# Two blocks of the first layer as one Strassen product in a retention, Mish and SwiGLU kernel

## The chip, the cores and the metric

The kernel runs on one core of a Trainium2 chip. The metric is the time of the program on the device in microseconds (us). Its engines work beside each other, each through its own list of instructions in order: TensorE (PE in the rows, with its weight loads as PEld), VectorE (DVE), ScalarE (ACT), GpSimd (POOL) and SyncE (SP), which issues the transfers (DMA) between the chip's memory and the core's SBUF. TensorE writes its products to PSUM, which has eight banks.

## The reference

What is computed, cut to the formulas. The retention is over 4 x 8 heads of 576 tokens; its output is the 2304 x 512 matrix `x` of the two layers behind it, which have 2048 and 1536 inner columns.

```python
ret = (scale * q @ k.T) * Dmat          # Dmat: gamma ** (i - j) below the diagonal
x = transposed(ret @ v)                 # 2304 tokens x 512
h = x @ w_in                            # first layer, 512 -> 2048
y = (h * tanh(log1p(exp(h)))) @ w_out   # Mish, 2048 -> 512
g = y @ w_gate                          # second layer, 512 -> 1536
out = (g * sigmoid(g) * (y @ w_val)) @ w_out2
```

## The kernel before

**Precision.** All products of the layers are of fp32 numbers in two parts, a high and a low one (type fp32r); a product is three matmuls: high x high, high x low, low x high. So every operand has to be split first: ScalarE copies the high part (a CAST), VectorE (sometimes GpSimd) subtracts it to get the low part. Weights come from memory as `raw` tiles of 128 x 512 64-bit words, out of which `rebias`, `sign` and `join` (lines 105 to 114: one operation of ScalarE, three of VectorE) make fp32 numbers.

**Stages.** The retention comes first, with the first slots of the first layer between its steps. The first layer works through six blocks of 384 tokens (`NB`, `T`); in each, 16 units of 128 inner columns (`F1`). `slot(s)` is unit `s % 16` of block `s // 16`: `g1` makes 12 matmuls of 128 x 384 into a bank `h`, ScalarE applies Mish and casts the high part of `g`, VectorE subtracts for the low part (`g_lo`, line 612), and `g2(s - 4)` makes the 12 matmuls of 128 x 384 of the slot four earlier (`LAG`) into four banks `acc`. A slot has 24 matmuls, and the first layer 96 slots. The weights of all 32 units stay in SBUF from the first block on.

**The second layer** takes two blocks as a pair and makes its first products by Strassen's method: seven products of sums and differences of quarters instead of eight. The quarters of its weights (12 groups of four quarters: `w_gate` and `w_val` in six pairs each) are made ahead, in the first layer's slots: `second(s)` runs one step of `group` and `last` a slot from slot 20 (`PREP`) on, in 14 of each 16 slots, five slots a group. A group loads two `raw` tiles, makes the numbers, forms four sums (line 213), and then `put`s seven quarters: cast, subtraction, and a store to DRAM (`comb`) from a tile `c`, of which there are four. `last` does the same with the second products' weights (`find`, two puts, the subtraction on GpSimd). All loads and stores stand on SP's list in the order of the program. In the second layer `stream` loads the quarters back (`su`), `ysteps` splits the seven combinations of a pair of blocks, and `strassen` makes the seven products of 6 matmuls each into three banks `t` that take turns in two; the second products (`fins`, 128 x 512) are spread between them.

Of the kernel before, what the change touches and what calls it, by code (L numbers as in the profile page):

```python
# [7 lines left out]
F32 = mybir.dt.float32  # L8
# [8 lines left out]
def retention_mish_swiglu(  # L17
# [28 lines left out]
    NA, NBU = 19, 13  # L46
# [3 lines left out]
    PREP = 20  # L50
    EARLY = (9, 11, 14, 17)
# [3 lines left out]
    cl, cr = ExitStack(), ExitStack()  # L55
    wa = cr.enter_context(tc.tile_pool(name="wa", bufs=NA, side="right"))
    dp = ctx.enter_context(tc.tile_pool(name="dp", bufs=1, space=bass.MemoryType.DRAM))
    gp = ctx.enter_context(tc.tile_pool(name="gp", bufs=3))
    xsp = cl.enter_context(tc.tile_pool(name="xsp", bufs=XS))
# [20 lines left out]

    def words(j):
        w = raw[j].rearrange("p (n t) -> p n t", t=2)
        return w[:, :, 0], w[:, :, 1]

    def fetch(lim):
# [5 lines left out]
        raw[j] = xp.tile([128, 2 * DM], U32, tag="raw", name=f"raw{j}", bufs=RAW)  # L91
# [24 lines left out]
    def part(lim, eng=nc.gpsimd):  # L116
# [5 lines left out]
        u = pools["a" if j < NA else "b"].tile([128, 2, DM], F32R, tag="u", name=f"u{j}")  # L122
# [48 lines left out]
    comb = [[dp.tile([128, 2, 2, KH], F32, tag=f"c{i}_{n}", name=f"comb{i}_{n}") for n in range(NG)] for i in range(PAIRS)]  # L171
    find = [dp.tile([128, 2, DM], F32, tag=f"f{i}", name=f"find{i}") for i in range(F2)]

    def raw_load(key, src, whole):
        raw[key] = xp.tile([128, 2 * DM], U32, tag="raw", name=f"raw{key}", bufs=RAW)
# [10 lines left out]
    def group(i, z, stg):  # L186
        keys = [f"{'gv'[z]}{i}_{e}" for e in range(2)]
        if stg == 0:
            for e in range(2):
                raw_load(keys[e], cols((w2_gate, w2_val)[z], 2 * i + e), False)  # L190
            return
        if stg == 1:
            for e in range(2):
                rebias_raw(keys[e])
            return
        if stg == 2:
            for e in range(2):
                sign(keys[e])
                join(keys[e])
            return  # L200
        v = {}
        for e in range(2):
            lo, hi = words(keys[e])
            for n in range(2):
                v[f"a{e + 1}{n + 1}"] = lo[:, n * KH:(n + 1) * KH].bitcast(F32)
                v["1324"[2 * e + n]] = hi[:, n * KH:(n + 1) * KH].bitcast(F32)
        s = {n: v[str(n)] for n in (1, 2, 3, 4)}
        if stg == 3:
            for out_, a, b, op in (
                (s[1], v["a21"], v["a22"], ALU.add), (s[3], v["a11"], v["a21"], ALU.subtract),  # L210
                (s[2], s[1], v["a11"], ALU.subtract), (s[4], v["a12"], s[2], ALU.subtract),
            ):
                nc.vector.tensor_tensor(out=out_, in0=a, in1=b, op=op)
        for c, nm in enumerate(USES):
# [708 lines left out]
```

## Time and profile before

| | us |
|---|---|
| median of three runs | 924.15 |
| lowest, highest | 924.09, 925.74 |
| the profiled execution | 925.63 |
| its span, first to last instruction | 923.5 |
| TensorE busy in it | 913.3 |
| VectorE, ScalarE, GpSimd busy | 514.5, 362.1, 75.5 |

An engine's busy time is the time in which at least one of its instructions runs. Matmuls overlap in a pipeline, so the mean time of one is longer than the step from one to the next. A row of windows gives, for a stretch of the span, the busy time of each engine, the granted clock of TensorE as a share of 2.4 GHz, the busy share of the DMA engines and what they moved.

### The profile page before, as it was taken

The page shows a single profiled execution, that of the slowest core. Times are in us where ns is not written, and L with a number is a line of the kernel's source. Part 1 is how long each engine was busy: PE and PEld are TensorE (multiplying, and loading weights), DVE is VectorE, ACT ScalarE, POOL GpSimd, SP SyncE. Part 2 cuts the span into 40 slices and gives each one's busy share as a digit, 9 for nine tenths or more (in the row PEclk, how much of TensorE's full clock was granted, in tenths as well). Part 3 has the DMA queues.
Part 4 walks back from the last instruction along what each step waited for, and adds up shares of the span by engine and source line. Part 5 has one row for each costly group of instructions (what it writes and reads, how often), then busy time and mean ns, then how long its engine had stood idle before and what let it go on. Part 6 is the DMA issues. An engine that isn't in the chain of part 4 may idle for free.

```text
span 923.5 us, 14629 instructions
## 1 busy us (share of the span) xinstructions
PE 913.3 (99%) x5684; PEld 870.5 (94%) x5684; DVE 514.5 (56%) x950; ACT 362.1 (39%) x729; POOL 75.5 (8%) x71
## 2 busy tenths in 40 slices
PE   9999999999999999999999999999999999999998
PEld 8888899999999999999999999998999998999997
DVE  3778599355656566656635444556444556544444
ACT  3767466344444445444533222223222223222222
POOL 3654200000000000000000000000000000000000
PEclk9999999999999999999999999999999999999999
DMA  9999255045554463454536755544644444644421
GB/s 206 253 247 250 70 180 185 23 149 171 171 171 155 158 198 130 164 189 127 181 138 224 254 206 205 205 160 161 226 160 157 156 162 155 216 158 160 160 69 69
DMA packets 115348, 156.56 MB, mean 170 GB/s; under 512 B 45392, under 2 KB 80976, under 8 KB 115280
## 3 DMA queue, kind: packets, MB, share of 16 engines
q1 hardware_dynamic: 114176, 155.21, 52.3%
q8 instruction: 45, 0.74, 0.3%
q10 hardware_dynamic: 1104, 0.42, 0.2%
q14 instruction: 23, 0.19, 0.1%
HBM read 122.58 MB, written 33.03 MB: 168 GB/s over the span
## 4 chain that ended last, share of the span: by engine, by line
PE 92%; DVE 3%; DMA 2%; ACT 2%; issue 1%; SPq 0%; ACTq 0%; DVEq 0%
PE t L816 28%; PE h L552 21%; PE acc L586 21%; PE fa L742 16%; PE o L455 2%; PE s L379 1%; DMA raw<-in_moe_w_out_dram 1%; DMA raw<-in_moe_w_in_dram 1%; PE idle L500 1%; PE tk L363 1%; PE o L446 1%; DVE p L388 1%; PE state L422 1%; PE tq L332 1%; DVE raw L114 0%
## 5 line engine op out<-in xcount | busy, mean ns | idle before, releaser
L816 PE MATMUL t<-y,su 128*128 128x384 f32 x1512 | 306.5, 338 | 1.0 <-DVE cv L783 1.0
L816 PEld LDWEIGHTS t<-y,su 128*128 128x128 f32 x1512 | 271.4, 188 | 24.4 <-DVE cv L783 2.3
L552 PE MATMUL h<-xs,u 128*128 128x384 f32 x1152 | 215.1, 336 | 0.0
L586 PE MATMUL acc<-g,u 128*128 128x384 f32 x1152 | 214.6, 336 | 0.3 <-DVE u L125 0.3
L586 PEld LDWEIGHTS acc<-g,u 128*128 128x128 f32 x1152 | 201.5, 188 | 0.6 <-DVE u L125 0.6
L552 PEld LDWEIGHTS h<-xs,u 128*128 128x128 f32 x1152 | 200.9, 188 | 0.4
L742 PE MATMUL fa<-fu,g 128*128 128x512 f32 x648 | 190.0, 395 | 0.1
L742 PEld LDWEIGHTS fa<-fu,g 128*128 128x128 f32 x648 | 118.6, 188 | 7.5 <-ACT g L764 0.5
L612 DVE TENSOR_TENSOR g<-m,g 128x384 fp32r<-128x384 f32 x96 | 53.7, 560 | 118.6 <-ACT g L608 118.2
L764 ACT CAST g<-sg 128x384 fp32r<-128x384 f32 x72 | 36.9, 513 | 175.0 <-DVE sg L801 121.4
L603 ACT ACTIVATE m<-h 128x384 f32<-128x384 f32 x96 | 47.0, 490 | 132.7 <-PE h L552 132.4
L790 ACT ACTIVATE sg<-sg 128x384 f32<-128x384 f32 x54 | 28.4, 525 | 96.3 <-DVE sg L783 96.3
L769 DVE TENSOR_TENSOR g<-sg,g 128x384 fp32r<-128x384 f32 x72 | 40.2, 558 | 40.6 <-ACT g L764 40.6
L182 POOL TENSOR_TENSOR f<-rawf,f 128x256 fp32r<-128x256 f32 x24 | 23.7, 1006 | 343.7 <-ACT f L181 343.7
L608 ACT CAST g<-m 128x384 fp32r<-128x384 f32 x96 | 49.4, 514 | 2.6
L783 DVE TENSOR_TENSOR u<-t,p 128x384 f32<-128x384 f32 x36 | 20.1, 557 | 49.8 <-PE t L816 45.6
L783 DVE TENSOR_TENSOR v<-t,p 128x384 f32<-128x384 f32 x36 | 20.0, 556 | 38.1 <-PE t L816 37.4
L801 DVE TENSOR_TENSOR sg<-sg,cv 128x384 f32<-128x384 f32 x54 | 30.2, 559 | 1.9
L114 DVE SCALAR_TENSOR_TENSOR raw<-raw 128x512 uint32<-128x512 uint32 x32 | 27.7, 866 | 0.0
L124 ACT CAST u<-raw 128x512 fp32r<-128x512 f32 x32 | 21.4, 669 | 13.9 <-DVE raw L114 13.8
L110 DVE SCALAR_TENSOR_TENSOR raw<-raw 128x512 uint32<-128x512 uint32 x32 | 26.0, 814 | 0.0
L105 ACT ACTIVATE raw<-raw 128x512 f32<-128x512 f32 x32 | 22.1, 689 | 9.0 <-DMA raw<-in_moe_w_in_dram 4.9
(80 smaller groups left out, 746.1 us busy)
## 6 DMA issues: line engine op xcount, KB each, us to landing
su<-comb SPq DMA_DIRECT2D x126, 512.0 KB, 3.2
comb<-c SPq DMA_DIRECT2D x84, 256.0 KB, 3.5
raw<-in_moe_w_in_dram SPq DMA_DIRECT2D x16, 512.0 KB, 5.1
raw<-in_moe_w_out_dram SPq DMA_DIRECT2D x16, 512.0 KB, 3.9
rawg<-in_moe_w_gate_dram SPq DMA_DIRECT2D x12, 512.0 KB, 6.2
rawf<-in_moe_w_out_dram SPq DMA_DIRECT2D x12, 512.0 KB, 4.7
rawv<-in_moe_w_val_dram SPq DMA_DIRECT2D x12, 512.0 KB, 6.4
find<-f SPq DMA_DIRECT2D x24, 256.0 KB, 2.4
```

Source lines behind the costliest of these rows:

```text
L552: nc.tensor.matmul(ps, lhsT=u[:, a, kk * 128:(kk + 1) * 128], rhs=s[:, e, :], start=(c == 0), stop=(c == n - 1),)
L586: nc.tensor.matmul(accs[b][d][:, :T], lhsT=u[:, a, d * 128:(d + 1) * 128], rhs=g[:, e, :], start=(i == 0 and c == 0), stop=(i == F1 - 1 an ...
L603: nc.scalar.activation(w, hs.pop(s), AF.Mish)
L608: nc.scalar.copy(out=gs[s][:, 0, :], in_=ws[s])
L612: nc.vector.tensor_tensor(out=g[:, 1, :], in0=ws.pop(s), in1=g[:, 0, :].bitcast(F32), op=ALU.subtract)
L742: nc.tensor.matmul(accs["f", b][m], lhsT=gs[u, e, h][:, x, m * 128:(m + 1) * 128], rhs=fu[2 * (u % PAIRS) + e][:, a, :], start=first, stop ...
L764: nc.scalar.copy(out=gs[u, e, h][:, 0, :], in_=x)
L769: nc.vector.tensor_tensor(out=g[:, 1, :], in0=x, in1=g[:, 0, :].bitcast(F32), op=ALU.subtract)
L783: nc.vector.tensor_tensor(out=out_, in0=a, in1=b_, op=ALU.add)
L790: nc.scalar.activation(x, bank_ if part_ is None else x, AF.Silu)
L801: later.append(lambda: nc.vector.tensor_tensor(out=y, in0=y, in1=x, op=ALU.mult))
L816: nc.tensor.matmul(p, lhsT=w[:, n % 2, a, kk * 128:(kk + 1) * 128], rhs=y[:, x, kk, :], start=begin and kk == 0 and (a, x) == (0, 0), stop ...
```

## The change

The first layer's slots stop after four blocks (`NC` = 4, 64 slots instead of 96). The last two blocks are one pair: `pair1(i)`, eight times, takes two units and makes seven Strassen products of 6 matmuls (128 x 384) into banks `te`, then Mish and the split of four results. The second products of a pair of units (`outs`) go into six banks `ea`: for each unit 36 matmuls of 128 x 256 (256 columns of one block, 256 of the other, the remaining 128 of both together) instead of 24 of 128 x 384. They stand in a queue, of which some are made after each Strassen product (`FIN1`); the second products of slots 60 to 63 (`old`) are made the same way during the first pair.

The quarters of the first layer's weights come from the units in SBUF: `group1` adds high and low parts, forms the four sums, puts four quarters through `c` tiles, and stores the other three (`ecomb`) from the unit itself. This preparation and the second layer's is one list (`pieces`): 14 pieces for each of the first eight groups, 10 for each of the last four, 2.6 pieces a slot from slot 20 on (`RATE`) and then 1.15 a Strassen product (`RATE1`). The combinations of the two blocks' tokens (`ye`) are made from slot 51 on, the last three in the first pair. Buffers of units that are no longer needed are taken again by name (`place`) for `ye`, the loaded quarters (`eu`, `su`), the second layer's combinations and its weights (`fu`).

```diff
-    NA, NBU = 19, 13
+    NA = 18
+    NC = 4
+    RATE, RATE1, AHEAD = 2.6, 1.15, 34
...
+    def place(kind, i, shape, dtype, name):
+        j = home[kind, i]
+        return pools["a" if j < NA else "b"].tile(shape, dtype, tag=f"u{j}", name=name)
...
+    def group1(i):
+        v = {}
+
+        def whole():
+            x = rp.tile([128, 2 * DM], U32, tag="raw", name=f"e{i}").bitcast(F32)
+            for e in range(2):
+                u = unit["in", 2 * i + e]
+                for h in range(2):
+                    nm = f"a{e + 1}{h + 1}"
+                    if nm in USES:
+                        m = i * NG + USES.index(nm)
+                        nc.sync.dma_start(
+                            out=comb1[m // 2][:, m % 2], in_=u[:, :, h * KH:(h + 1) * KH].bitcast(F32)
+                        )
+                    v[nm] = x[:, (2 * e + h) * KH:(2 * e + h + 1) * KH]
+                nc.vector.tensor_tensor(
+                    out=x[:, e * DM:(e + 1) * DM], in0=u[:, 0, :].bitcast(F32), in1=u[:, 1, :].bitcast(F32),
+                    op=ALU.add,
+                )
...
+        for n in range(2 * PAIRS):
+            load, bias, whole, sums, puts = gr[n]
+            f_load, f_bias, f_whole, f_puts = last(n)
+            g = group1(n) if n < F1 // 2 else None
+            yield bias
+            yield lambda: (whole(0), f_load())
+            if g:
+                yield g[0]
+            yield lambda: whole(1)
+            if g:
+                yield g[1]
+            yield sums
+            yield lambda: puts(("a11", "a12", "a22"))
+            if g:
+                yield lambda: g[2](("s2", "s3"))
+            yield lambda: puts(("s2", "s3"))
+            yield lambda: (puts(("s1", "s4")), gr[n + 1][0]() if n + 1 < 2 * PAIRS else None)
+            if g:
+                yield lambda: g[2](("s1", "s4"))
+            yield f_bias
+            yield f_whole
+            yield f_puts
...
+            if s >= PREP:
+                second(int((s + 1 - PREP) * RATE))
...
+            for c, (nm, tn, begin) in enumerate(PRODUCTS):
+                if begin:
+                    t[tn] = pha.tile([128, T], F32, tag="h", name=f"te{i}_{tn}")
+                p = t[tn]
+                m = i * NG + c
+                product(p, su["e", m // 2][:, m % 2], ys["e", c], begin)
+                if m % 2:
+                    stream1(m // 2 + len(ring1))
+                new = []
+                if c == 0:
+                    nc.scalar.copy(out=r["p1"], in_=p)
+                elif c == 1:
+                    add(r["u"], p, r["p1"])
+                elif c == 2:
+                    result(0, 0, wt("w"), p)
+                elif c == 3:
+                    r["v"] = wt("v")
+                    add(r["v"], p, r["p1"])
+                else:
+                    e, h, x = ((1, 1, r.get("v")), (1, 0, r["p1"]), (0, 1, r["u"]))[c - 4]
+                    add(x, p, x)
+                    result(e, h, x, x)
+                fins(FIN1[c] if i else 6)
+                while rests:
+                    rests.pop(0)()
+                rests.extend(new)
+                step = i * NG + c
+                if i == 0:
+                    pop(ahead, 2)
+                elif step >= AHEAD:
+                    pop(ahead, 1)
+                second(int((NS - PREP) * RATE + (step + 1) * RATE1))
+
+        FIN1 = (9, 12, 12, 12, 9, 9, 9)
...
+            if s == NS - F1 + 2:
+                ya, yb = ysteps("e", xt[NB - 2], xt[NB - 1])
+                ahead += ya + yb[0] + yb[1]
+            if s > NS - F1 + 2:
+                pop(ahead, 1 + s % 2)
```

The order on VectorE at slots 62 to 64 before (L612 is `g_lo` of a slot, L262 the low part of the next block's tokens, L213 sums and L182 puts of a group):

```order
L612 TENSOR_TENSOR g62_3974<-m62_3972,g62_3974 128x384
L612 TENSOR_TENSOR g63_4008<-m63_4002,g63_4008 128x384
L262 TENSOR_TENSOR xs4_2_4004<-x4_1172,xs4_2_4004 128x384
L262 TENSOR_TENSOR xs4_3_4006<-x4_1172,xs4_3_4006 128x384
L213 TENSOR_TENSOR rawv3_0_3857<-rawv3_1_3859 128x256
L213 TENSOR_TENSOR rawv3_0_3857<-rawv3_0_3857,rawv3_1_3859 128x256
L213 TENSOR_TENSOR rawv3_1_3859<-rawv3_0_3857 128x256
L213 TENSOR_TENSOR rawv3_1_3859<-rawv3_0_3857,rawv3_1_3859 128x256
L182 TENSOR_TENSOR c3_7_4017<-rawv3_0_3857,c3_7_4017 128x256
L182 TENSOR_TENSOR c3_9_4021<-rawv3_0_3857,c3_9_4021 128x256
L182 TENSOR_TENSOR c3_12_4025<-rawv3_1_3859,c3_12_4025 128x256
L612 TENSOR_TENSOR g64_4056<-m64_4054,g64_4056 128x384
```

And in the changed kernel, from the `g_lo` of slot 61 to that of slot 62 and on (L677 is `g_lo`, the tile of two slots bears the even number; L192 are puts of both kinds, L770 the low part of a token combination):

```order
L677 TENSOR_TENSOR g60_4130<-m61_4173,g60_4130 128x384
L192 TENSOR_TENSOR c3_7_4177<-rawv3_0_3961,c3_7_4177 128x256
L192 TENSOR_TENSOR c3_9_4181<-rawv3_0_3961,c3_9_4181 128x256
L192 TENSOR_TENSOR c3_12_4185<-rawv3_1_3963,c3_12_4185 128x256
L192 TENSOR_TENSOR e7_s2_4189<-e7_4087,e7_s2_4189 128x256
L192 TENSOR_TENSOR e7_s3_4193<-e7_4087,e7_s3_4193 128x256
L192 TENSOR_TENSOR c3_8_4197<-rawv3_1_3963,c3_8_4197 128x256
L192 TENSOR_TENSOR c3_10_4201<-rawv3_0_3961,c3_10_4201 128x256
L770 TENSOR_TENSOR ye_3_1_4142<-x5_1404,ye_3_1_4142 128x384
L677 TENSOR_TENSOR g62_4235<-m62_4233,g62_4235 128x384
L192 TENSOR_TENSOR c3_11_4238<-rawv3_0_3961,c3_11_4238 128x256
L192 TENSOR_TENSOR c3_13_4242<-rawv3_1_3963,c3_13_4242 128x256
```

Seven puts in a row now stand between two slots' `g_lo`, where there were three or four, and parts of the token combinations come between them.

ScalarE behind the Mish of slot 63, before (L603 Mish, L608 the high part of `g`, L257 of the tokens, L181 casts of puts):

```order
L603 ACTIVATE m63_4002<-h63_3977 128x384
L257 CAST xs4_2_4004<-x4_1172 128x384
L257 CAST xs4_3_4006<-x4_1172 128x384
L608 CAST g63_4008<-m63_4002 128x384
L181 CAST c3_7_4017<-rawv3_0_3857 128x256
L181 CAST c3_9_4021<-rawv3_0_3857 128x256
L181 CAST c3_12_4025<-rawv3_1_3859 128x256
L603 ACTIVATE m64_4054<-h64_4041 128x384
```

And in the changed kernel, into the first pair (L666 Mish, L673 the high part of `g`, L114 rebias of a raw tile, L191 casts of puts, L921 the copy of the first Strassen product out of its bank, L766 the high part of a token combination, L897 Mish of a result):

```order
L666 ACTIVATE m63_4285<-h63_4260 128x384
L673 CAST g62_4235<-m63_4285 128x384
L114 ACTIVATE rawf7_4085<-rawf7_4085 128x512
L191 CAST f7_0_4293<-rawf7_4085 128x256
L191 CAST f7_1_4297<-rawf7_4085 128x256
L921 COPY scratch_4303<-te0_1_4304 128x384
L766 CAST ye_4_0_4318<-x4_1202 128x384
L766 CAST ye_4_1_4319<-x4_1202 128x384
L114 ACTIVATE rawg4_0_4246<-rawg4_0_4246 128x512
L114 ACTIVATE rawg4_1_4248<-rawg4_1_4248 128x512
L766 CAST ye_5_0_4344<-t2_e_3811 128x384
L897 ACTIVATE we0_4360<-te0_1_4304 128x384
```

The copy that frees the first bank, and the Mish that frees it again, stand behind preparation work that waits for VectorE, for stores and for loads.

## Rows read from the trace of the kernel before

**Rows 1.** Page: busy time of PE, and its granted clock in 40 slices

```profile
PE 913.3 (99%) x5684; PEld 870.5 (94%) x5684; DVE 514.5 (56%) x950; ACT 362.1 (39%) x729; POOL 75.5 (8%) x71
PEclk9999999999999999999999999999999999999999
```

**Rows 2.** Windows: first layer (first row), second layer (second row)

```profile
core 0: us, PE busy (x) PEld busy (x) DVE busy (x) ACT busy (x) POOL busy (x), PEclk, DMA share, GB/s
300.00:400.00 100.00, 100.00 (x577) 100.00 (x577) 59.54 (x117) 49.67 (x108) 8.22 (x9) 1.00 0.49 162
600.00:700.00 100.00, 99.49 (x514) 91.90 (x514) 50.46 (x94) 25.47 (x49) 0.00 (x0) 1.00 0.49 174
```

**Rows 3.** Timeline of PE in the second layer: start, duration, line, shape, count

```profile
702.05 1.22 PE L816 MATMUL t<-y,su 128*128 128x384 f32 x6
703.10 0.86 PE L742 MATMUL fa<-fu,g 128*128 128x512 f32 x3
703.80 1.22 PE L816 MATMUL t<-y,su 128*128 128x384 f32 x6
```

**Rows 4.** Timeline of PE in the retention: full weights, narrow products

```profile
82.97 1.00 PE L446 MATMUL o<-qT,sbd 128*128 128x64 f32 x8
83.91 0.68 PE L455 MATMUL o<-p,vs 64*64 64x64 f32 x16
```

**Rows 5.** Groups of VectorE: line, form, count, busy us, mean ns, idle before

```profile
L612 DVE TENSOR_TENSOR g<-m,g 128x384 fp32r<-128x384 f32 x96 | 53.7, 560 | 118.6 <-ACT g L608 118.2
L182 DVE TENSOR_TENSOR c<-rawv,c 128x256 fp32r<-128x256 f32 x42 | 16.5, 422 | 7.3 <-ACT c L181 7.3
L125 DVE TENSOR_TENSOR u<-raw,u 128x512 fp32r<-128x512 f32 x19 | 13.1, 688 | 1.7 <-ACT u L124 0.9
L262 DVE TENSOR_TENSOR xs<-x,xs 128x384 fp32r<-128x384 f32 x18 | 11.8, 678 | 0.0
L110 DVE SCALAR_TENSOR_TENSOR rawg<-rawg 128x512 uint32<-128x512 uint32 x12 | 10.4, 869 | 0.0
L596 DVE COPY y<-acc 128x384 f32<-128x384 f32 x12 | 6.5, 554 | 6.4 <-PE acc L586 6.3
L213 DVE TENSOR_TENSOR rawg<-rawg,rawg 128x256 f32<-128x256 f32 x12 | 5.1, 423 | 0.2
L106 DVE TENSOR_SCALAR rawg<-rawg 128x512 uint32<-128x512 uint32 x12 | 5.0, 427 | 9.1 <-DMA rawg<-in_moe_w_gate_dram 9.1
```

**Rows 6.** Tile c: its idle-ended lines and landing time of its stores

```profile
  DMA comb<-c: 13.6, 22
DMA to landing us min/median/max: 2.0/3.5/5.9
```

**Rows 7.** Timeline of one group's last puts: the third and fourth wait for stores

```profile
313.94 1.32 SPq L183 DMA_DIRECT2D comb<-c  x3
315.59 0.95 ACT L181 CAST c<-rawv 128x256 fp32r<-128x256 f32 x2
316.77 0.42 ACT L181 CAST c<-rawv 128x256 fp32r<-128x256 f32 x1 [0.23 <-DMA comb<-c]
317.22 0.42 DVE L182 TENSOR_TENSOR c<-rawv,c 128x256 fp32r<-128x256 f32 x1 [0.23 <-ACT c L181]
317.85 0.42 ACT L181 CAST c<-rawv 128x256 fp32r<-128x256 f32 x1 [0.66 <-DMA comb<-c]
```

**Rows 8.** Page, DMA issues: KB each, median us from issue to landing

```profile
comb<-c SPq DMA_DIRECT2D x84, 256.0 KB, 3.5
rawg<-in_moe_w_gate_dram SPq DMA_DIRECT2D x12, 512.0 KB, 6.2
```

**Rows 9.** Groups of ScalarE

```profile
L608 ACT CAST g<-m 128x384 fp32r<-128x384 f32 x96 | 49.4, 514 | 2.6
L181 ACT CAST c<-rawg 128x256 fp32r<-128x256 f32 x42 | 16.2, 423 | 7.4 <-DMA comb<-c 6.0 <-DVE c L182 0.6 <-issue 0.5
```

More of the change, by code (lines that the diff above doesn't have):

```diff
@@ L219, in last, with whole @@
[L219 to L225 removed]
+        def whole(e):
+            sign(keys[e])
+            join(keys[e])
+            lo, hi = words(keys[e])
+            for h in range(2):
+                v[f"a{e + 1}{h + 1}"] = lo[:, h * KH:(h + 1) * KH].bitcast(F32)
+                v["s" + "1324"[2 * e + h]] = hi[:, h * KH:(h + 1) * KH].bitcast(F32)
@@ L226, in last, with whole, puts @@
+    def last(i):
+        key = f"f{i}"
+        def whole():
             sign(key)
             join(key)
-        else:
+        def puts():
             x = words(key)[0].bitcast(F32)
@@ new lines, in product, with add @@
+        def product(p, w, y, begin):
+            for kk in range(KT // 2):
+                for a, x in ((0, 0), (0, 1), (1, 0)):
+                    nc.tensor.matmul(
+                        p, lhsT=w[:, a, kk * 128:(kk + 1) * 128], rhs=y[kk][:, x, :],
+                        start=begin and kk == 0 and (a, x) == (0, 0), stop=kk == KT // 2 - 1 and a == 1,
+                        skip_group_check=True,
+                    )
+        def add(out_, a, b_):
+            nc.vector.tensor_tensor(out=out_, in0=a, in1=b_, op=ALU.add)
@@ new lines, in old, with one @@
+        def old(s):
+            u, g, b = unit["out", s % F1], gs.pop(s), s // F1
+            def one(d, a, e, stop, last_):
+                nc.tensor.matmul(
+                    accs[b][d][:, :T], lhsT=u[:, a, d * 128:(d + 1) * 128], rhs=g[:, e, :], start=False, stop=stop
+                )
+                if last_:
+                    g2_out(s)
+            i = s % F1
+            e_ = order(KT, i == F1 - 1)
+            for n, (d, a, e, c) in enumerate(e_):
+                finq.append(lambda d=d, a=a, e=e, c=c, n=n: one(d, a, e, i == F1 - 1 and c == 2, n == len(e_) - 1))
@@ L721, in retention_mish_swiglu @@
+        second(10 ** 6)
+        cr.close()
+        pools["sg"] = ctx.enter_context(tc.tile_pool(name="sg", bufs=5, side="right", reuse_waits="tile"))
+        pools["sx"] = ctx.enter_context(tc.tile_pool(name="sx", bufs=2, side="right", reuse_waits="tile"))
+        for n in range(len(ring1), len(ring2)):
             stream(n)
+        later += rests
         fin_load(0)
```

365 lines of the change are left out of this document (223 added, 142 removed).

## The prediction

> **What bounds the kernel now.** I read the page first: TensorE is busy for 913.3 of 923.5 us at the full granted clock in all but the edges [rows 1]. Then windows inside the two layers: in the first layer TensorE is busy for all of 100 us and starts 577 matmuls in it, one every 173.3 ns; VectorE is busy for 59.54 us and ScalarE for 49.67 [rows 2]. In the second layer TensorE is busy for 99.49 of 100 us. So the time is the number of matmuls by their step, as long as nobody makes TensorE wait. The reader is to keep both in mind: what the change takes from TensorE, and how much work it puts on the engines that now have some 40% to spare.
>
> **What the change takes from TensorE.** It removes 32 slots of 24 matmuls, 768 x 173.3 ns = 133.1 us. It adds 8 pairs x 42 = 336 matmuls of 384 columns in sevens as the second layer has them. There, six of them take 1.05 us from their first start to the next line's (702.05 to 703.10), 175 ns each, and three of 512 columns 0.70 us (703.10 to 703.80), 233 ns each [rows 3]: 336 x 175 = 58.8 us. The third part is 16 units x 36 = 576 matmuls of 256 columns, which no row shows. By columns, or by the straight line through 384 and 512, one is 117 ns. From the other side, products of only 64 columns with a full load of weights come every 0.94 / 8 = 118 ns (82.97 to 83.91) [rows 4], so the weights set a floor near the same number. I take 117 ns: 67.4 us. Saved: 133.1 - 58.8 - 67.4 = 6.9 us. Bounds: at 110 ns 10.9 us saved; at 140 ns, if loading and streaming of nearly equal length hinder each other, 6.4 us lost.
>
> **What it puts on VectorE and ScalarE in the slots.** The order up to slot 19 is the same on every engine, so only slots 20 to 63 count. A slot is 24 x 173.3 ns = 4.16 us. VectorE's own work in one is a `g_lo` of 0.56 us and a sixteenth of four token splits of 0.68 and two copies of 0.55, in all 0.80 us [rows 5]. Of the 59.54 us in 100 [rows 2], 24.0 slots x 0.80 = 19.2 are this; the rest is 24.0 x 14/16 / 5 = 4.2 groups, 9.6 us each. The new part of a group is two additions of 512 columns and eight operations of 256: 2 x 0.69 + 8 x 0.42 = 4.7 us [rows 5]. The 14 pieces of such a group take 14 / 2.6 = 5.4 slots, 22.4 us, and hold 9.6 + 4.7 + 5.4 x 0.80 = 18.6 us of VectorE: 83%.
>
> That leaves 3.8 us, and the puts claim them. A put needs one of four tiles from its cast (0.42 us [rows 9]) over the subtraction (0.42 [rows 5]) to the landing of its store, 3.5 us in the median [rows 6, 8]: 4.35 us for four, 1.09 us each. Of 13 puts in a group 11 stand in five consecutive pieces, 8.0 us of slots. Four find a tile free, seven come every 1.09 us: 4 x 0.42 + 7 x 1.09 = 9.3 us, in which VectorE works for 11 x 0.42 + 2 x 0.56 = 5.7. So about 3.6 us of waiting a group, against 13.6 us in the whole kernel now, where three and four puts stand in two slots and only the last two wait [rows 6, 7]. With 22.2 of 22.4 us the slots hold, just. The landing ranges from 2.0 to 5.9 us [rows 6]: 1.0 to 8.5 us of waiting. The wait for a group's loads, 9.1 us in 12 groups [rows 5], adds up to 0.8. From slot 51 to 63, 54.1 us, come 16 further halves of token combinations on VectorE, some 0.56 us each, 9.0 us, and eight casts on ScalarE: VectorE is then about 9 us late when the slots end. What is queued behind is `g_lo` and the Mish of the next slot, but TensorE needs a slot's `g` only four slots later, 16.6 us. So nothing of this shows before slot 64.
>
> By the Trainium skill, page "DMA: Bandwidth & Descriptors", section "Anatomy of one DMA — SWDGE (gpsimd) path", a transfer that GpSimd issues takes some 2.0 us plus its bytes at 436 GB/s, which would be an estimate of 2.6 us for 256 KB. The fastest store here, 2.0 us, is below that, but the median of SP's stores, 3.5 us, is well above it [rows 6]. With 2.6 us a put would cost 0.86 us, a group 1.6 us less, and VectorE would be some 5 us late instead of 9; the sum goes by the row.
>
> **Where it shows: the first pair.** Here TensorE needs VectorE and ScalarE at once. The third product adds onto the first one's bank, which ScalarE must have copied; the fourth onto the second's, which VectorE must have read. Between a product's end and the one after next lie two portions of six old matmuls and a product, 1.04 + 1.05 + 1.04 = 3.1 us. TensorE's own work in the pair is 42 x 175 + 42 x 173.3 ns = 14.6 us. VectorE's list holds in it: three operations of the last `find` tile (0.43 + 2 x 0.87), six halves of combinations (3.4), two rebias operations (0.85), four of sign and join (3.5), four sums (1.7), seven puts (2.9), five additions (2.8), two low parts (1.1) [rows 5]: 18.4 us, 3.8 more than TensorE's. With 9 us of delay brought along and 3.1 of slack, TensorE waits 9 + 3.8 - 3.1 = 9.7 us. In the next four pairs a step is 1.05 + 10.3 x 0.117 = 2.25 us, a pair 15.8 us, and VectorE has 0.8 x 9.6 + 9 x 0.56 = 12.7 us. Seven puts stand in three pieces; at 3.5 us to landing this holds, at 5.9 it costs 1 to 1.5 us a group. I put 1.3 us there, 0 to 6. The last three pairs have no preparation beside them.
>
> **Edits at nothing.** The extra transfers (4.7 MB of stores and loads a pair of units) lie on DMA engines that are 0.49 busy [rows 2]; the first quarters are asked for six slots ahead. If that cover went, VectorE would wait for loads of 6.2 us [rows 8], which is in the bounds. Buffers taken by name are free before their new owner writes them, since their last matmul is slots or pairs earlier; otherwise SP's list would hold back stores behind them. The second layer keeps its order, and its first unit makes the last 256-column products where it had few others.
>
> **The sum.** Against the profiled execution: 925.63 - 6.9 + 9.7 + 1.3 = 929.7 us. That execution took 1.5 us more than the median of 924.15, so the median goes to 928.2 us.
>
> **Rivals.** (1) The other side: the engines keep up. If stores land in 2 to 3 us, the slots lose 1 to 2 us a group instead of 3.6, ScalarE and VectorE end slot 63 within a bank's slack, and only the 3.8 us of the first pair count against 3.1: 924.15 - 6.9 + 1.5 = 918.8 us. For it: 40% of VectorE are idle now [rows 2], and the last stores of a group wait no more than 0.66 us [rows 7]. Against it: the tighter bursts. The point where it decides is a delay of some 6 us at slot 64. (2) The delay grows over all eight groups. At 5.9 us to landing a group needs 27 us of VectorE in 22.4, the delay passes 16.6 us before slot 64, and TensorE waits in the slots already: some 8 x 4.7 + 9 - 16.6 = 30 us at the worst, half of it likelier: 924.15 - 6.9 + 11 + 15 = 943 us. (3) The change doesn't do what it says: a matmul of 256 columns does not get cheaper in proportion. At 140 ns and no wait beyond rival 1's, 932 us; at the 175 ns of 384 columns, 952 us. Against it: 118 ns are what full weights cost with few columns [rows 4]. (4) Between the forecast and rival 1: 4 to 8 us of waiting eat the gain, 922.3 to 926.
>
> **How the numbers follow.** The forecast with its neighbourhood, 926 to 936 us: 0.42. Rival 1, under 922.3: 0.33. Rival 4: 0.12. Rival 2: 0.08. Rival 3: 0.05. About 0.2%, 1.85 us, is what a measurement can tell from no change. Faster: 0.33; the same: 0.12; slower: 0.42 + 0.08 + 0.05 = 0.55. The range is 917.5 to 939 us: below it lies only the case of no wait with less than 117 ns, above it most of rivals 2 and 3. The likeliest case's own range is 926 to 936.
>
> **What would show it.** Right: TensorE's idle time in the first layer stands at the product line of the first pair, released by the copy on ScalarE and the additions on VectorE, some 10 us in 25; `g_lo` of slots 56 to 63 runs later and later behind its matmuls; casts of puts wait for stores several us a group; matmuls of 256 columns step at 117 ns; before slot 64 TensorE has no holes. Wrong: TensorE full through the first pair (rival 1), holes in the slots (rival 2), a step over 125 ns (rival 3), or the waits in the later pairs instead of the first.

## The result and the profile after

The changed kernel takes **936.78 us** in the median (935.03 to 938.14), the kernel before in the same comparison 924.55 us: a ratio of **1.0129, 95% interval 1.0109 to 1.0150**. It is slower by some 12 us, where 928.2 us was forecast with a range of 917.5 to 939. The profiled execution took 935.03 us with a span of 933.2 us, 9.7 us more than the span before.

The page of the changed kernel, TensorE's row and three groups (line, operation, form, count, busy us, mean ns, idle before):

```profile
PE 910.6 (98%) x5828; PEld 863.5 (93%) x5828; DVE 568.0 (61%) x1086; ACT 380.0 (41%) x798; POOL 70.0 (8%) x71
L615 PE MATMUL h<-xs,u 128*128 128x384 f32 x768 | 144.0, 337 | 0.7 <-DVE xs L325 0.7
L649 PE MATMUL acc<-g,u 128*128 128x384 f32 x720 | 135.0, 336 | 3.8 <-ACT y L659 3.5
L813 PE MATMUL te<-ye,eu 128*128 128x384 f32 x336 | 69.8, 343 | 9.3 <-ACT scratch L921 6.1
```

Against [rows 1], TensorE is busy for 2.7 us less while the span is 9.7 us longer. It now waits in all three groups: the second products of the slots (L649, 3.8 us), the first products of the slots (L615, 0.7) and the seven products of the merged part (L813 te, 9.3). The windows of the changed kernel show where; the first two are in the slots, the third and fourth in the first pair:

```profile
core 0: us, PE busy (x) PEld busy (x) DVE busy (x) ACT busy (x) POOL busy (x), PEclk, DMA share, GB/s
240.00:260.00 20.00, 17.91 (x103) 17.41 (x102) 14.56 (x31) 12.06 (x28) 1.45 (x2) 1.00 0.83 277
290.00:320.00 30.00, 27.85 (x158) 27.00 (x157) 21.26 (x48) 16.70 (x41) 1.46 (x2) 1.00 0.76 244
363.00:372.00 9.00, 2.94 (x17) 2.62 (x16) 5.58 (x12) 5.73 (x14) 0.83 (x2) 0.83 0.94 297
372.00:395.00 23.00, 21.09 (x109) 19.12 (x110) 17.82 (x38) 13.40 (x31) 2.07 (x3) 0.92 0.90 315
```

Where the kernel before had TensorE full for 100 of 100 us [rows 2], these windows lose 2.1, 2.2, 6.1 and 1.9 us. In none of them is VectorE or ScalarE full: 17.82 of 23 us is the densest. In the 9 us in which TensorE all but stands still, each of them works for under 6. So neither is short of time; each of them waits in its own order.

**The slots.** TensorE's timeline in the changed kernel, around the three holes before slot 64 (start, duration, line, form, count, idle before and what ended it):

```profile
243.75 2.47 PE L649 MATMUL acc<-g,u 128*128 128x384 f32 x12 [2.09 <-ACT y L659]
...
296.03 3.23 PE L615 MATMUL h<-xs,u 128*128 128x384 f32 x17 [0.73 <-DVE xs L325]
...
313.27 2.47 PE L649 MATMUL acc<-g,u 128*128 128x384 f32 x12 [1.43 <-ACT y L659]
```

The first and the third stand where a block of tokens ends: the next block's second products go into the same four banks, which ScalarE and VectorE must have copied out (`y`, L659). The second stands where the next block's split tokens (`xs`) are due. ScalarE's timeline just ahead of the first hole shows what held the copy:

```profile
240.60 0.41 ACT L191 CAST e_s<-e 128x256 fp32r<-128x256 f32 x1 [4.38 <-DMA comb<-c]
...
242.29 0.48 ACT L666 ACTIVATE m<-h 128x384 f32<-128x384 f32 x1
242.81 0.51 ACT L673 CAST g<-m 128x384 fp32r<-128x384 f32 x1
243.23 0.85 ACT L659 COPY y<-acc 128x384 f32<-128x384 f32 x2
```

A put's cast stands for 4.38 us, until the store of an older put has landed and its tile is free; in the kernel before, the two such waits shown were of 0.23 and 0.66 us [rows 7]. Two more puts (left out here), the slot's Mish and its cast come next, and the bank's copy is behind all of them.

**The first pair.** TensorE's timeline over its first products (`te`, with portions of the old second products between):

```profile
361.37 1.21 PE L813 MATMUL te<-ye,eu 128*128 128x384 f32 x6
...
364.51 1.21 PE L826 MATMUL acc<-g,u 128*128 128x384 f32 x6
371.78 2.29 PE L813 MATMUL te<-ye,eu 128*128 128x384 f32 x6 [6.06 <-ACT scratch L921]
373.87 2.04 PE L826 MATMUL acc<-g,u 128*128 128x384 f32 x6
375.75 1.22 PE L813 MATMUL te<-ye,eu 128*128 128x384 f32 x6
...
383.58 1.28 PE L813 MATMUL te<-ye,eu 128*128 128x384 f32 x6 [1.07 <-issue]
```

The third product waits 6.06 us for ScalarE's copy of the first one's bank. When it runs, its six matmuls take 2.09 us from start to next line and the six old ones 1.88, where 1.05 and 1.04 are usual: the granted clock is 0.83 and 0.92 in these windows, so part of the time runs at the lower of the two levels (1.2 instead of 2.4 GHz). That costs 1.9 us more. ScalarE and VectorE in the same stretch:

```profile
352.74 0.75 ACT L191 CAST c<-rawv 128x256 fp32r<-128x256 f32 x2
...
361.82 0.41 ACT L191 CAST e_s<-e 128x256 fp32r<-128x256 f32 x1 [4.91 <-DMA comb<-c]
...
370.62 0.73 ACT L191 CAST f<-rawf 128x256 fp32r<-128x256 f32 x2 [1.92 <-DVE rawf L123]
371.26 0.47 ACT L921 COPY scratch<-te 128x384 f32<-128x384 f32 x1
...
357.92 0.43 DVE L201 TENSOR_TENSOR rawv<-rawv,rawv 128x256 f32<-128x256 f32 x1
...
359.20 1.08 DVE L192 TENSOR_TENSOR c<-rawv,c 128x256 fp32r<-128x256 f32 x3
...
368.17 0.56 DVE L677 TENSOR_TENSOR g<-m,g 128x384 fp32r<-128x384 f32 x1 [0.51 <-ACT g L673]
```

Slot 63's first product started at 357.21 us and its `g_lo` runs at 368.17, 10.96 us later; where nothing is late that distance is 3.35 us (slots 20 to 23 of this trace). So VectorE comes 7.6 us late out of the slots.

**Where the loss is.** I measured four stages by the starts of TensorE's lines: from slot 20's first product to slot 63's; the first pair; the other seven; layer 2's first unit. The first experiment, which has the same matmuls and no preparation beside them, gives what each takes unhindered:

| kernel | slots 20 to 63 | first pair | other seven pairs | first unit of layer 2 | median us |
|---|---|---|---|---|---|
| no engine work in the preparation | 179.18 | 14.62 | 111.20 | 27.11 | 915.65 |
| changed kernel | 184.49 | 24.85 | 115.32 | 27.16 | 936.78 |

The difference is 5.3 us in the slots, 10.2 in the first pair and 4.1 in the others, 19.6 of the 21.1 us between the two.

### The profile page after: what moved, and what is told of

The parts are those of the page before. It is cut to its first block, busy times and chain, and to the rows that moved or that the text cites. A ratio compares the mean times of both kernels' runs of the same rounds, so it can differ in the third digit from the quotient of the medians.

```text
span 933.2 us, 15315 instructions
## 1 busy us (share of the span) xinstructions
PE 910.6 (98%) x5828; PEld 863.5 (93%) x5828; DVE 568.0 (61%) x1086; ACT 380.0 (41%) x798; POOL 70.0 (8%) x71
## 4 chain that ended last, share of the span: by engine, by line
PE 72%; DMA 10%; DVE 10%; ACT 4%; issue 2%; SPq 1%; POOL 0%; DVEq 0%; ACTq 0%; POOLq 0%
PE t L813 28%; PE fa L989 16%; PE h L615 7%; PE acc L649 6%; PE ea L855 5%; PE te L813 4%; DMA comb<-c 3%; DMA rawg<-in_moe_w_gate_dram 2%; DMA eu<-ecomb 2%; DMA rawv<-in_moe_w_val_dram 1%; PE o L518 1%; DMA raw<-in_moe_w_out_dram 1%; PE s L442 1%; DVE c L192 1%; DVE g L677 1%
## 5 line engine op out<-in xcount | busy, mean ns | idle before, releaser
L813 PE MATMUL t<-y,su 128*128 128x384 f32 x1512 | 306.3, 338 | 0.5 <-DVE cv L820 0.5
L813 PEld LDWEIGHTS t<-y,su 128*128 128x128 f32 x1512 | 270.6, 188 | 23.7 <-DVE cv L820 1.9
L615 PE MATMUL h<-xs,u 128*128 128x384 f32 x768 | 144.0, 337 | 0.7 <-DVE xs L325 0.7
L649 PE MATMUL acc<-g,u 128*128 128x384 f32 x720 | 135.0, 336 | 3.8 <-ACT y L659 3.5
L615 PEld LDWEIGHTS h<-xs,u 128*128 128x128 f32 x768 | 133.9, 188 | 1.5 <-DVE xs L325 1.0
L649 PEld LDWEIGHTS acc<-g,u 128*128 128x128 f32 x720 | 125.5, 188 | 5.2 <-ACT y L659 4.2
L813 PE MATMUL te<-ye,eu 128*128 128x384 f32 x336 | 69.8, 343 | 9.3 <-ACT scratch L921 6.1
L855 PE MATMUL ea<-ge,u 128*128 128x256 f32 x576 | 78.1, 282 | 0.2 <-ACT y L659 0.2
L855 PEld LDWEIGHTS ea<-ge,u 128*128 128x128 f32 x576 | 75.6, 189 | 0.9 <-DVE y L659 0.4
L813 PEld LDWEIGHTS te<-ye,eu 128*128 128x128 f32 x336 | 57.5, 191 | 11.5 <-ACT scratch L921 6.4
L677 DVE TENSOR_TENSOR g<-m,g 128x384 fp32r<-128x384 f32 x64 | 36.1, 565 | 36.7 <-ACT g L673 36.5
L666 ACT ACTIVATE m<-h 128x384 f32<-128x384 f32 x64 | 31.0, 485 | 38.0 <-PE h L615 37.9
L192 POOL TENSOR_TENSOR f<-rawf,f 128x256 fp32r<-128x256 f32 x24 | 18.9, 811 | 337.7 <-ACT f L191 267.2
L673 ACT CAST g<-m 128x384 fp32r<-128x384 f32 x64 | 32.9, 514 | 1.8
```

The lines of the kernel that those rows point to most:

```text
L615: nc.tensor.matmul(ps, lhsT=u[:, a, kk * 128:(kk + 1) * 128], rhs=s[:, e, :], start=(c == 0), stop=(c == n - 1),)
L649: nc.tensor.matmul(accs[b][d][:, :T], lhsT=u[:, a, d * 128:(d + 1) * 128], rhs=g[:, e, :], start=(i == 0 and c == 0), stop=(i == F1 - 1 an ...
L666: nc.scalar.activation(w, hs.pop(s), AF.Mish)
L673: nc.scalar.copy(out=gs[s][:, 0, :], in_=ws[s])
L677: nc.vector.tensor_tensor(out=g[:, 1, :], in0=ws.pop(s), in1=g[:, 0, :].bitcast(F32), op=ALU.subtract)
L813: nc.tensor.matmul(p, lhsT=w[:, a, kk * 128:(kk + 1) * 128], rhs=y[kk][:, x, :], start=begin and kk == 0 and (a, x) == (0, 0), stop=kk == ...
```

## The experiments

Twelve kernels, in the order in which they ran. The kernel before ran beside each of them (924.35 to 924.86 us).

**No engine work in the preparation.** The loads, VectorE's and ScalarE's work and the casts of the preparation go; the stores stay, from a unit that lies there (so what layer 2 and the merged part multiply is not the right numbers).

```diff
-        c = pools["c"].tile([128, 2, KH], F32R, tag="c", name=nm)
-        nc.scalar.copy(out=c[:, 0, :], in_=x)
-        eng.tensor_tensor(out=c[:, 1, :], in0=x, in1=c[:, 0, :].bitcast(F32), op=ALU.subtract)
-        nc.sync.dma_start(out=dst, in_=c.bitcast(F32))
+        nc.sync.dma_start(out=dst, in_=unit["out", F1 - 1][:, :, :KH].bitcast(F32))
```

> The changed kernel with the preparation's work on VectorE, ScalarE and GpSimd and its loads left out from slot 20 on; its stores stay, from a tile of a unit, so later weights are not the reference's. All matmuls stay. Theory A (TensorE waits for engines that preparation keeps late): the holes go, 5.3 us in the slots, 10.2 in the first pair, 4.2 in the later ones, so 936.8 - 19.7 = 917 us, 915 to 920. Rival B (the matmuls themselves are dearer than forecast, 256 columns or the mixing of two kinds): 930 us or more.

Measured: 915.65 us, ratio 0.9904 (0.9889 to 0.9919). The change's gain on TensorE is there in full, and all of its loss comes from what is left out here: the engines' work and the loads of the preparation.

**Three staging tiles instead of four.**

```diff
-        pools["c"] = cr.enter_context(tc.tile_pool(name="pc", bufs=4, side="right"))
+        pools["c"] = cr.enter_context(tc.tile_pool(name="pc", bufs=3, side="right"))
```

> The changed kernel with three tiles for puts instead of four; same work, same order. Theory A1 (the delay comes from casts that wait for a put tile's store): a put in a burst costs a third instead of a quarter of a cycle of some 4 us, 0.3 us more, seven or eight puts in each of 12 groups: 15 to 30 us more, 950 to 967 us. Theory A2 (the delay comes from the amount of VectorE's work alone, which fills the slots): within 3 us of 936.8.

Measured: 964.57 us, ratio 1.0444 (1.0424 to 1.0463); slots 200.72, first pair 35.13, the others 116.89. One tile less costs 27.8 us. The waits (waiting engine and tile, what it waited for: us, times, longest) of the changed kernel:

```profile
ACT e_s L191 <- DMA comb<-c: 33.6, 15, 4.9
...
PE te L813 <- ACT scratch L921: 6.1, 1, 6.1
```

and of this one:

```profile
ACT e_s L191 <- DMA comb<-c: 47.6, 27, 7.5
PE te L813 <- ACT scratch L921: 16.5, 1, 16.5
...
PE h L615 <- ACT xs L320: 9.4, 2, 8.0
```

The casts' waits for a tile grow, and with them TensorE's first wait in the pair and new ones for the tokens' splits. So the ring of tiles is on the path.

**The puts one by one between other work.** The same work in the same four tiles, but each of a group's eleven puts is a piece of its own, three of them ahead of the sums and two between the steps of the `find` tile, instead of five pieces in a row that hold two or three each; the rates rise with the count of pieces (from 14 and 10 a group to 20 and 14).

```diff
+            yield lambda: whole(1)
+            yield lambda: puts(("a11",))
             if g:
                 yield g[0]
-            yield lambda: whole(1)
+            yield lambda: puts(("a12",))
             if g:
                 yield g[1]
+            yield lambda: puts(("a22",))
             yield sums
-            yield lambda: puts(("a11", "a12", "a22"))
+            yield lambda: puts(("s2",))
             if g:
-                yield lambda: g[2](("s2", "s3"))
-            yield lambda: puts(("s2", "s3"))
+                yield lambda: g[2](("s2",))
+            yield lambda: puts(("s3",))
...
```

> The changed kernel with the same preparation in another order: puts one by one between additions, sums and the steps of the last tile, instead of eleven in five pieces; 20 smaller pieces for 14 (rate 3.68 a slot for 2.6, 1.61 a product for 1.15), so the same groups in the same slots. Theory A1 (waits for put tiles): most of the delay goes, the slots' 5.3 us and half or more of the first pair's 10.2: 925 us, 922 to 929. Theory A2 (amount of work): 934 to 938 us.

Measured: 928.25 us, ratio 1.0040 (1.0025 to 1.0055); slots 179.18, first pair 20.47, the others 116.88. The holes in the slots are gone to the last tenth, with VectorE's work the same. What is left, 5.9 and 5.7 us, is in the pairs.

**One group of seven puts later.** In the changed kernel's order, seven instead of eight groups in the slots (2.37 pieces a slot instead of 2.6), the eighth in the pairs.

> The changed kernel with one of the second layer's groups (9.6 us of VectorE, nine puts) moved from the slots to the pairs: rate 2.37 a slot for 2.6, the first layer's quarters all still in the slots. Theory A in both forms: the delay at slot 64 falls by some 10 us, the slots' holes and most of the first pair's go (12 us less), the later pairs get 2 to 5 us more: 929 us, 926 to 933. If the first pair's waits come from its own list alone and not from a delay brought along: 936 to 940.

Measured: 936.71 us, ratio 1.0133 (1.0118 to 1.0148); slots 181.23, first pair 27.37, the others 115.96. A miss of 8 us: the slots gained the 3.3 us that less work brings, and the first pair lost 2.5 again. I put that down to the end of the slots' list, where the sixth group's puts and two quarters' now stand in a row; it was not tried apart.

**Half the rate in the pairs.** One number of the changed kernel:

```diff
-    RATE, RATE1, AHEAD = 2.6, 1.15, 34
+    RATE, RATE1, AHEAD = 2.6, 0.62, 34
```

> Changes one number: the 32 pieces of preparation that are left when the pairs begin are given out at 0.62 a product instead of 1.15, so that they last to the eighth pair instead of the fourth; the slots are those of the changed kernel. Theory A, a pair loses time by the preparation that stands in its own queues (3.8 us of VectorE in the first pair) besides the lateness it inherits: the first pair's 10.2 us fall by half of that list, to about 8.3, the 4.2 us of the later pairs to about 1.5; time about 932 (930 to 934). Theory B, only what comes late out of the slots counts, and the later pairs' waits are an echo of the first: pairs as in the changed kernel, 936.8 +- 1.5.

Measured: 941.02 us, ratio 1.0179 (1.0156 to 1.0202); slots 184.70, first pair 22.68, the others 111.20, and layer 2's first unit 36.94. By stages theory A holds: 2.2 us less in the first pair, and the other seven as without any preparation. The 9.8 us at layer 2's start I had not foreseen. With 40 pieces left (not 32, as I had counted) at 0.62 a product, some are still there when the last product is out. TensorE in this kernel:

```profile
498.90 1.58 PE L855 MATMUL ea<-ge,u 128*128 128x256 f32 x12
508.14 2.29 PE L813 MATMUL t<-y,su 128*128 128x384 f32 x6 [7.66 <-ACT p L1061]
```

and ScalarE, where the left pieces' casts and the load of a new table stand ahead of the copy that layer 2 waits for:

```profile
505.56 0.74 ACT L191 CAST f<-rawf 128x256 fp32r<-128x256 f32 x2 [1.83 <-DVE rawf L123]
506.32 1.28 ACT L977 ACT_TABLE_LOAD   x1
507.61 0.48 ACT L1061 COPY p<-t 128x384 f32<-128x384 f32 x1
```

**Nothing in the first pair.** The changed kernel, with no piece given out during the first seven products:

```diff
-                second(int((NS - PREP) * RATE + (step + 1) * RATE1))
+                second(int((NS - PREP) * RATE + max(0, step - 6) * RATE1))
```

> No piece of preparation during the seven products of the first pair; the pieces left follow from the second pair on at the old rate. Theory A (the prediction's split of the first pair's wait: 9 inherited, 3.8 from the pair's own list): the first pair's 24.85 us fall by 3.8 to about 21, and the later pairs' 4.2 us grow by 0 to 2 since the list moves there: 934 (932 to 936). Theory B (all of it inherited): first pair 24.5 to 25, time 936.8 or more. Theory C (all of it the pair's own list): first pair 15 to 17, time 928 to 930.

Measured: 935.26 us, ratio 1.0108 (1.0091 to 1.0125); slots 185.76, first pair 23.12, the others 116.09. The first pair lies between theories A and B: its own list was worth 1.7 us, not 3.8; 8.5 us are inherited or follow from what is. (The fifth experiment, with only half of that list gone, won 2.2, so the figure is good to some half a microsecond.) The list came back in the fourth and sixth pair (17.21 and 19.43). In the sixth it stands beside layer 2's token combinations, which begin with product 34; what makes the fourth longer was not tried.

**Spread, and half the rate.** The third experiment's order, its 57 last pieces at 1.1 a product instead of 1.61.

> The kernel with the puts spread between other work (928.25 us, slots without holes, 12.4 us lost in pairs 0 to 4), and its pieces left at the pairs' start given out at 1.1 a product instead of 1.61, so over all eight pairs. Theory A: the loss is in proportion to what of the list a pair carries once its queues are not late: 5.9 us of the first pair fall to 4, the other 6.5 us to about 2; time 922 (919 to 925), as fast as the kernel before or faster. Theory B: the loss is the same wherever the work stands: 928 +- 1.

Measured: 922.32 us, ratio 0.9975 (0.9964 to 0.9987); slots 179.18, first pair 19.84, the others 111.96. The later pairs' loss is one of density. In the first pair ScalarE's timeline shows the bank's copy once more behind a put, whose tile is free only when an older store, 5.91 us under way, has landed:

```profile
362.05 0.40 ACT L191 CAST e_s<-e 128x256 fp32r<-128x256 f32 x1 [2.30 <-DMA ecomb<-e_s]
362.36 0.47 ACT L929 COPY scratch<-te 128x384 f32<-128x384 f32 x1
```

**Spread, and more in the slots.** The same order at 4.2 pieces a slot instead of 3.68, and 0.68 in the pairs.

> The kernel with the puts spread, 4.2 pieces a slot instead of 3.68 (185 pieces by the last slot instead of 162) and 0.68 a product in the pairs, so about half of the list there. Theory A: VectorE was busy 78 to 87% in the slots with the spread order; with 14% more pieces it is at 89 to 99% in the densest stretch, so a few holes come back (2 to 4 us) while the pairs lose 3 to 5 us instead of 12.4: 923 (919 to 928). Theory B: the slots cannot take more (as with the first order, where 83% was already late by a group): holes of 6 us or more and a late first pair, 930 to 936.

Measured: 943.43 us, ratio 1.0204 (1.0188 to 1.0219); slots 194.18, first pair 27.63, the others 111.20. Theory B, and worse than it said. TensorE at the first block's end in this kernel:

```profile
246.16 3.33 PE L657 MATMUL acc<-g,u 128*128 128x384 f32 x12 [3.19 <-ACT y L667]
```

There is an edge between 3.68 and 4.2 pieces a slot, beyond which the same hole opens that the bunches opened.

**Half the rate again, in time.** The fifth experiment with 0.8 instead of 0.62.

> As the half-rate kernel, at 0.8 a product instead of 0.62, so that the last piece (the run at 0.62 left some pieces behind the last product, and layer 2's first unit took 36.9 us instead of 27.2) is made within the eighth pair. Theory A (the later pairs' waits come from the density of their own list; the slots' holes and the inherited lateness stay): slots 184.7, first pair 22.5 to 23.5, all later pairs 15.9 to 16.2, layer 2's first unit 27.2: 931 (930 to 933). If the 9.8 us at layer 2's start had another cause than the late pieces: 939 to 942.

Measured: 931.44 us, ratio 1.0077 (1.0062 to 1.0092); slots 185.18, first pair 23.71, the others 112.00, layer 2's first unit 27.16. The first pair and the second (16.67) are 0.2 and 0.5 us over theory A's ranges. So the late pieces made the 9.8 us, and the density of the pairs' list was 3.3 of the changed kernel's 4.1 us.

**Spread, from slot 18, and room around the border.** Begun two slots earlier, through but for one piece by slot 61, nothing in the first four products:

```diff
-    PREP = 20
+    PREP = 18
...
-    RATE, RATE1, AHEAD = 2.6, 1.15, 34
+    RATE, RATE1, AHEAD = 3.68, 1.2, 34
...
-                second(int((s + 1 - PREP) * RATE))
+                second(min(162, int((s + 1 - PREP) * RATE)))
...
-                second(int((NS - PREP) * RATE + (step + 1) * RATE1))
+                second(int(162 + max(0, step + 1 - 4) * RATE1))
```

> The spread order at 3.68 pieces a slot, begun two slots earlier (slot 18, where VectorE was busy 7.1 of 14 us) and so through with the 162 pieces two slots earlier; none in slots 62 and 63 and in the first four products; then 1.2 a product. Theory A (the first pair's remaining 5.2 us and the second's 0.8 stem from pieces queued ahead of its copies and additions, inherited or its own): slots 179.2, first pair 15 to 17, time 918.5 (917 to 921). Theory B (what remains there is the pair's own chain from product to y and back): first pair 19 to 20, time 922 +- 1. If the earlier start collides with the last weights of the first layer: 923 to 926.

Measured: **915.89 us, ratio 0.9912 (0.9895 to 0.9929)**; slots 179.18, first pair 14.62, the others 111.21; 1.1 us under theory A's range. That is the time without any engine work in the preparation, with all of it done, and 8.5 us under the kernel before. A window of its slots and one of its first pair, TensorE from slot 63 into the pair, and VectorE's `g_lo` of slot 63:

```profile
174.00:350.00 176.00, 176.00 (x1016) 176.00 (x1015) 139.00 (x301) 95.34 (x223) 10.93 (x14) 1.00 0.75 249
356.00:371.00 15.00, 15.00 (x88) 15.00 (x88) 9.45 (x19) 7.16 (x16) 0.40 (x1) 1.00 0.90 340
```

```profile
352.18 2.24 PE L623 MATMUL h<-xs,u 128*128 128x384 f32 x12
...
356.34 1.21 PE L821 MATMUL te<-ye,eu 128*128 128x384 f32 x6
...
358.44 1.21 PE L821 MATMUL te<-ye,eu 128*128 128x384 f32 x6
```

```profile
355.95 0.87 DVE L685 TENSOR_TENSOR g<-m,g 128x384 fp32r<-128x384 f32 x1 [0.87 <-ACT g L681]
```

VectorE is busy for 139.00 of 176 us, 79%, and TensorE has no hole. Slot 63's `g_lo` comes 355.95 - 352.18 = 3.77 us after its first product, 0.4 late. The second row also answers a rival, that the transfers themselves are short of room in the first pair, where the changed kernel's DMA engines are 0.94 and 0.90 busy: here they are 0.90 busy at 340 GB/s, a quarter's store issued at 352.55 us takes 7.36 us to land, and TensorE does not wait, since no cast that needs such a store's tile stands ahead of its copies.

**Spread, denser, then free.** The same room, bought with 3.86 pieces a slot from slot 20.

> The same two free slots and four free products, bought by 3.86 pieces a slot from slot 20 instead of an earlier start. Theory A (3.68 left room, only 4.2 did not): slots 179 to 180, first pair 15 to 17: 919 (917.5 to 921). Theory B (3.68 is already the limit, so 5% more opens holes at the blocks' ends, as 14% more did with 15 us): slots 182 to 186 and time 923 to 928.

Measured: 915.99 us, ratio 0.9910 (0.9895 to 0.9925), the same stages (1.5 us under theory A's range). So what counts is the room at the border, not how it was bought, and the edge that the eighth experiment met lies between 3.86 and 4.2 pieces a slot. The two parts of the room, two slots and four products, were not tried apart.

**The pace alone.** The changed kernel's own bunches, with the pace of the tenth experiment: from slot 18 at 2.6 a slot, at most 114 pieces by slot 63, then 0.87 a product from the fifth on.

> The changed kernel's own order of pieces (puts in bunches of four to eight), with the pace of the fastest kernel so far: from slot 18 at 2.6 a slot, none in slots 62 and 63 nor in the first four products, then 0.87 a product. Theory A (the bunches open the slots' holes, the pace near the end makes the first pair): slots 183 to 185, first pair 15 to 19, all else unhindered: 922 to 926. Theory B (the lateness at the slots' end is the same 8 to 9 us wherever the list ends, since puts drain no faster): first pair 21 to 24: 928 to 931. If the slots' holes go as well (under 180 us), the order of the puts never mattered and the pace alone was at fault: 916 to 918.

Measured: 920.76 us, ratio 0.9956 (0.9940 to 0.9973); slots 183.45, first pair 14.88, the others 111.21. The holes in the slots stay, and the rest of the loss goes; the time is 1.2 us under theory A's range. TensorE's timeline in this kernel:

```profile
242.30 2.61 PE L649 MATMUL acc<-g,u 128*128 128x384 f32 x12 [0.97 <-ACT y L659]
294.70 3.27 PE L615 MATMUL h<-xs,u 128*128 128x384 f32 x17 [0.71 <-DVE xs L325]
...
312.60 1.77 PE L649 MATMUL acc<-g,u 128*128 128x384 f32 x8 [0.52 <-DVE y L659]
...
355.84 2.24 PE L615 MATMUL h<-xs,u 128*128 128x384 f32 x12
```

and VectorE's `g_lo` of slot 63:

```profile
363.94 0.56 DVE L677 TENSOR_TENSOR g<-m,g 128x384 fp32r<-128x384 f32 x1 [0.21 <-ACT g L673]
```

It comes 363.94 - 355.84 = 8.10 us after its product, 4.8 late, and the first pair loses only 0.26 us. So a lateness of about 5 us at slot 64 is hidden where no put stands in the pair's queues. The order of this kernel differs from the tenth's in more than the puts: the steps of the `find` tile stand in a row too, and the cast ahead of the first hole's copy waits here 1.91 us for VectorE's numbers of that tile and not for a put's tile.

The last three and the changed kernel share the loss out: the order in bunches makes the holes in the slots (4.3 to 5.3 us; none once the pieces are spread), and the pace around the border and in the pairs makes the rest (10.2 and 4.1 us; 0.26 and nothing once there is room).

## Why the prediction was right, and where it was not

The direction held, and so did the place and the kind of the first pair's wait; the part on the slots failed, and the size was short by 8.6 us.

- **TensorE's own gain, 6.9 us: 6.2 to 7.9.** The kernel without engine work is 8.8 us under the kernel before, the tenth 8.5. From slot 20 on the tenth's profiled execution is 7.9 us shorter, of which 6.2 lie in the stages that the change touches. The 256-column matmul steps at (408.73 - 407.31) / 12 = 118 ns in the rows here, 117 was taken, so the third rival is out:

```profile
407.31 1.58 PE L855 MATMUL ea<-ge,u 128*128 128x256 f32 x12
408.73 1.23 PE L813 MATMUL te<-ye,eu 128*128 128x384 f32 x6
```

- **VectorE's lateness at slot 64, 9 us: 7.6 measured** at slot 63, by other parts. The load came near (83% of a group's slots forecast, 79% in the tenth experiment's slots). But the sum let the slots up to 51 "hold, just" and put the 9 us to the token combinations behind them. In the trace `g_lo` is already 2.7 us late at slot 25, 4.8 at slot 35 and 4.1 at slot 51, so the puts cost more than they were priced at. The rows had a store land in 3.5 us [rows 6]; in the changed kernel the landings out of the same four tiles are, for the 84 stores of the second layer's quarters (`c`) and the 32 of the first layer's (`e_s`):

```profile
DMA to landing us min/median/max: 2.0/2.4/5.0
DMA to landing us min/median/max: 2.0/4.4/7.5
```

  The 2.6 us that the prediction worked out from the Trainium skill, page "DMA: Bandwidth & Descriptors", section "Anatomy of one DMA — SWDGE (gpsimd) path", an estimate for another engine's queue, lie near the first of these medians and far below the second.
  A tile was not held by the store alone. The prediction let its time be cast, subtraction and landing, one after the other, 4.35 us; it left out that the subtraction queues on VectorE behind everything else there while ScalarE stands. The timelines of the first pair's stretch show it: a tile cast at 352.74 us is subtracted at 359.20, behind the sums of the next quarters; the put that needs the tile has waited since 356.91 and casts at 361.82, 9.1 us after the tile was taken. From a cast's start to its store's landing the trace has 5.5 us in the median of the 95 puts begun in slots 20 to 63, and 9.9 at most; the kernel before had 5.1 and 8.0 there.
- **"TensorE needs a slot's `g` only four slots later. So nothing of this shows before slot 64": this step failed**, and cost 5.3 us (184.49 us of slots where 179.18 were due). It is true of `g`. But ScalarE's and VectorE's queues also hold the copies that empty a block's banks and the next block's splits, and these TensorE needs at once. The slack of four slots is that of one customer of the queue, not of the queue.
- **First pair, 9.7 us: 10.2 measured, by other parts.** The first wait stands where it was forecast (the copy of the first product's bank). The pair's own list was worth 1.7 us instead of 3.8 (sixth experiment), and 1.9 us are the lower clock behind the hole, which the sum did not price. That the two numbers lie so near is in part luck.
- **Later pairs, 1.3 us: 4.1 measured**, within the 0 to 6 given. The list's density made 3.3 of it (ninth experiment).
- **The extra transfers, put at nothing,** are no cause by themselves (tenth experiment), but they lengthen what a put waits for. The DMA engines were 0.68 busy in the changed kernel's slots (window 174 to 350 us) and 0.90 to 0.94 in its first pair, not 0.49. The stores of `find` landed in 4.5 us in the median, where the kernel before had 2.4. In the third and the seventh experiment the cast ahead of the first bank's copy waits for a quarter's store that takes 6.72 and 5.91 us. The transfers come to 29.4 MB in all by the two pages, 3.7 a pair of units and not 4.7.
- **The first rival, engines that keep up, 918.8 us,** was to decide at "a delay of some 6 us at slot 64". Where nothing is given out in the first products, the runs bear that out: 4.8 us at slot 63 cost 0.26 in the twelfth experiment, 7.2 us cost 8.5 in the sixth. But the delay alone does not decide. The third experiment is 2.3 us late at slot 63 and loses 5.9 in the first pair, the seventh 3.4 and 5.2, because a put stands ahead of the bank's copy. The second rival's holes in the slots came, without its growth: lateness rose in the slots to 8 us, not past 16.6.
- **Two sums do not come out.** At 5.9 us to landing the prediction's own formula gives 4 x 0.42 + 7 x 1.69 - 5.7 = 7.8 us of waiting a group, not 8.5, so the second rival's worst case is some 24 us instead of 30. And the first pair makes three low parts, not two, 0.6 us more on VectorE's list. Neither changes the forecast's side.

The forecast of 929.7 us for the profiled execution's own time thus lacked 5.3 us in the slots, 2.8 in the later pairs and 0.5 in the first; against these stand some 1.0 us more between the kernel before and one without waits from slot 20 on, and 2.1 us that the profiled execution of the changed kernel was ahead at slot 20, before the change begins to work. It took 935.03.

What stays open: of the 7.9 us gained between the profiled executions of the kernel before and the tenth experiment from slot 20 on, 1.6 us lie in layer 2 behind its first unit, whose instructions the change does not touch. Two steps between units, of 0.91 us each before and 0.65 and 0.67 in the tenth, make 0.5 of it; the rest is spread over some 2000 steps. And why a first layer's quarter takes longer to land than a second layer's out of the same tiles was not tried.

## What to carry to other kernels

Ask of an engine that serves the bottleneck not only how late its usual result may come, but which of the customers of its queue is the most impatient, and where in the program that one stands: here the banks at a block's end and the first pair of a new phase. Work that waits for a resource of its own (few staging tiles, each held from a cast through a queued subtraction to a store's landing) should be dealt out singly between other work, and its list should end some slots ahead of a border at which TensorE needs the same engines at once. Both cost no instruction here, and turned 1.3% slower into 0.9% faster than the kernel before.

## What the runs showed of the hardware

- After a hole of 6 us TensorE came back at the lower clock level: twelve matmuls of 384 columns took 2.09 + 1.88 us where 1.05 + 1.04 are usual, with a granted clock of 0.83 and 0.92 in the two windows around them. This hole cost 1.9 us more than its length.
- A matmul of 256 columns with a full load of weights steps at 118 ns, the same as one of 64 columns in the retention [rows 4].
- VectorE at 79% and the 16 DMA engines at 0.75, 249 GB/s, left TensorE without a hole for 176 us, with the puts dealt out singly (tenth experiment). In the changed kernel the same window has VectorE at 129.17 of 176 us, 73%, and the three holes.
